# Attention and GEGLU block in one kernel: the last two groups in units of two head slots by 128 queries, and the first half of the last FFN beside the last exponentials

## The chip, the cores and the metric

The kernel runs on one core of a Trainium2 chip. The metric is the device time of one execution in microseconds (us). The engines are named as the profile names them: PE is TensorE (PEld its weight loads), DVE is VectorE, ACT is ScalarE, POOL is GpSimd, SP is the engine that issues DMAs.

## The reference

x has 2048 tokens of 512 bf16 values; 32 heads of 16; the FFN is 1792 wide.

```python
def _A_ref(x, wqkv, wo):                      # S = 2048, D = 512, H = 32, Dh = 16
    qkv = (x @ wqkv).reshape(B, S, 3, H, Dh).transpose(2, 0, 3, 1, 4)
    q, k, v = qkv[0], qkv[1], qkv[2]
    scores = jnp.einsum("bhqd,bhkd->bhqk", q, k) * (Dh ** -0.5)
    p = softmax(scores, axis=-1)
    o = jnp.einsum("bhqk,bhkd->bhqd", p, v)
    return o.transpose(0, 2, 1, 3).reshape(B, S, D) @ wo

def _B_ref(x, w_gate, w_up, w_down):
    return (gelu(x @ w_gate) * (x @ w_up)) @ w_down      # tanh form of Gelu

h  = x + _A_ref(layernorm(x), A_wqkv, A_wo)
h2 = h + _B_ref(layernorm(h), B_w_gate, B_w_up, B_w_down)
return h2
```

## The kernel before, in words

**A plan in Python.** Every instruction is recorded by `P.op` or `P.dma` (lines 96 and 112) with the buffers that it reads and writes; the plan works out the semaphore waits. So the order of the calls in Python is the order of each engine's queue, and what a queue holds is executed in that order.

**Groups, slots, units.** The 2048 queries are cut into eight groups of 256 tokens (`gi`), the 32 heads into eight slots of four heads (`slot`). A unit `ui` is one group and one slot, 64 in all (line 345). The four heads of a slot stand on four groups of 32 partitions, so that score matmuls use 32 rows of the PE array each, at tile positions 0, 32, 64 and 96.

**Two passes and the tick.** Softmax needs each row's maximum ahead of the exponential. In pass 1 (`p1_pair`, line 831, `p1_consume`, line 847) PE makes the scores with queries on partitions, two banks of 128x512 at a time, and DVE reduces them to maxima (L856); that pair is a *tick*, and a unit has 16 ticks. The negated maximum is written by `negm_pre` and `negm_post` (lines 878 and 894), through one DMA transpose per unit and one POOL addition (L905), into unused rows of the query operand. In pass 2 (`p2_tile`, line 914) PE makes the scores again, with keys on partitions: per unit eight key pairs `m` by four heads `g`, each a bank of two 256-wide matmuls (L921), from which ACT takes exp (L950, or in pairs of banks L938). Pass 2 is 24 ticks behind pass 1 (`P2_START`, line 982). After the last tick of pass 1 (1024) there are thus 24 ticks with pass 2 alone; here `dve_free` is set and DVE does the evacuations. `item_pv` (line 953) multiplies the exponentials by V, in four pieces from ticks 15 to 18 of a unit (`PV_T`): heads on four groups of 32 PSUM partitions, 17 columns each, the last one of which sums the row. The result goes through a DMA transpose (`o_turn`) and is divided on POOL (`o_norm`: L998, L1002).

**The dense stream.** All other matmuls are items in a queue (`Dense`, line 528): `prio` for what is due, `ready` for the rest, and `piece()` gives out one piece per tick, whose cost is counted in 512-wide matmuls. `startable` and `act_lag` hold an item back while ACT is thought to be late. If a tick's piece is under two such matmuls, `dummy` (L1410) fills the rest; in the last 24 ticks five in every two ticks are filled (`FILL_2`, line 1524). When all slots of a group are done, `post_onT` transposes the group's output, `item_oproj` does the out-projection and the residual, POOL the LayerNorm (`ln2_from_sums`), `post_hnT` transposes, and `add_ffn` queues seven `item_gate` and seven `item_up` (two chunks of 128 FFN columns by 256 tokens, L1198) and two `item_down` (L1250 and L1255). ACT evacuates gate and up; Gelu is a polynomial on POOL and a tanh on ACT (`gelu_chain`, L1178 and L1186 to L1190, the product L1242). A group's FFN runs while the next group's scores are worked on.

**The end.** The last group has no next one. `tail_a` (line 1275) transposes the first six slots of its output, `item_ofin` (line 1009) treats slot 6, and `tail_b` (line 1350) does the rest behind the last exponential: `tail_norm` and `tail_onT` for slot 7, the out-projection of both token tiles (L1361), statistics (L1364, L1365, L1369), reciprocal root on POOL (L1373), normalisation (L1375), transposes (`tail_hnT`), with up to 13 matmuls put in by `fill(FILL_LN)`, which are those of a queued `item_down` of group 6; then all seven gate and up tiles for 256 tokens with a real Gelu on ACT (L1211) and the product on DVE (L1227), the downs two steps behind, and the two stores (L1406).

## Time and profile before

| | |
|---|---|
| median of 3 runs | 1231.28 us (1231.07 to 1231.67) |
| the profiled execution's own time | 1231.23 us |
| its span, first to last instruction | 1229.3 us |
| last row maximum of pass 1 ends | 1176.8 us |
| last exponential ends | 1200.1 us |
| first gate matmul of the last FFN | 1207.85 us |
| busy share of the span | PE 90%, DVE 96%, ACT 97%, POOL 68% |

The times in the profile count from the span's start. A line number such as L856 is that of the kernel before. Matmul records hold the whole way through the array, so what a matmul costs in a row of many is read from the distance of their starts. "x8" in a row is eight instructions merged; the first number is the first one's start and the second the time up to the last one's end.

### The profile page before, as it was taken

What the parts mean: (1) busy time and instruction counts of PE and PEld (TensorE: products, weight loads), DVE (VectorE), ACT (ScalarE), POOL (GpSimd) and SP (SyncE); (2) the same over time, 40 slices, a digit from 0 to 9 for tenths busy, and PEclk for the clock granted to TensorE, in tenths of its full rate; (3) what the DMA queues carried; (4) which work ended last, traced back from release to release, by engine and by line L of the source; (5) the groups of instructions that cost most, each with busy time, mean ns of one, the idle gap of its engine ahead of it and who ended that gap; (6) DMA issues with size and microseconds to landing.
All of it is one profiled execution on the core that took longest, in us unless ns stands there. A gap on an engine that the chain in (4) does not pass through costs nothing.

```text
span 1229.3 us, 31435 instructions
## 1 busy us (share of the span) xinstructions
PE 1104.8 (90%) x12462; PEld 429.5 (35%) x12598; DVE 1175.8 (96%) x1111; ACT 1189.5 (97%) x2417; POOL 834.6 (68%) x1760
## 2 busy tenths in 40 slices
PE   7899988889998989898989989999888988889898
PEld 3233232233333333333332333333333333333335
DVE  8999999999999999999999999999999999999933
ACT  7899999999999999999999999999999999999993
POOL 7567684766776586757768477775867777548850
PEclk9999999999999999999999999999999999999999
DMA  4111114200010000100011000100001100010000
GB/s 153 27 34 27 29 26 136 87 10 9 8 27 21 14 9 8 31 21 7 11 25 18 17 11 7 28 21 13 10 8 26 27 8 11 18 32 10 8 19 14
DMA packets 68658, 31.54 MB, mean 26 GB/s; under 512 B 53920, under 2 KB 67488, under 8 KB 68512
## 3 DMA queue, kind: packets, MB, share of 16 engines
q1 hardware_dynamic: 68512, 29.52, 9.5%
q8 instruction: 101, 1.65, 0.5%
q14 instruction: 45, 0.37, 0.1%
HBM read 11.80 MB, written 2.10 MB: 11 GB/s over the span
## 4 chain that ended last, share of the span: by engine, by line
ACT 57%; DVE 29%; PE 8%; issue 3%; POOL 2%; DMA 0%; POOLq 0%; DVEq 0%
ACT PTM L950 32%; DVE PM L856 29%; ACT PTG L950 10%; ACT PTE L950 6%; PE pbank L1250 2%; ACT g_sb L685 2%; ACT u_sb L685 2%; ACT th_sb L1178 2%; PE pbank L841 1%; PE pbank L921 1%; PE pbank L1198 1%; ACT OB L685 1%; PE pbank L443 1%; DVE OA L853 1%; PE pbank L1410 1%
## 5 line engine op out<-in xcount | busy, mean ns | idle before, releaser
L856 DVE TENSOR_REDUCE PM<-pbank 128x2 f32<-128x1024 f32 x998 | 1135.9, 1212 | 8.3 <-PE pbank L921 3.8
L950 ACT ACTIVATE PTM<-pbank 128x512 bf16<-128x512 f32 x1357 | 731.9, 719 | 3.9 <-PE pbank L921 0.4
L921 PE MATMUL pbank<-QT,KT 32*128 32x256 bf16 x4096 | 503.0, 273 | 14.8 <-ACT PTM L950 7.6
L841 PE MATMUL pbank<-KT,QT 32*128 32x512 bf16 x2022 | 388.6, 384 | 31.5 <-DVE PM L856 11.8
L1410 PE MATMUL pbank<-ones_bf,ident 128*128 128x512 bf16 x708 | 221.4, 384 | 52.2 <-ACT PTM L950 22.5
L950 ACT ACTIVATE PTG<-pbank 128x512 bf16<-128x512 f32 x407 | 224.8, 704 | 1.7 <-PE pbank L921 1.3
L841 PEld LDWEIGHTS pbank<-KT,QT 32*128 32x128 bf16 x2022 | 97.9, 90 | 363.4 <-DVE PM L856 139.0
L921 PEld LDWEIGHTS pbank<-QT,KT 32*128 32x128 bf16 x4096 | 170.3, 92 | 75.9 <-ACT PTM L950 40.4
L950 ACT ACTIVATE PTE<-pbank 128x512 bf16<-128x512 f32 x236 | 139.3, 717 | 1.3 <-PE pbank L921 0.9
L964 PE MATMUL pbank<-PTM,VA 128*17 128x256 bf16 x2776 | 125.4, 274 | 1.5
L998 POOL TENSOR_TENSOR LINV<-OBT,negone 128x8 f32<-128x8 bf16 x62 | 103.5, 1670 | 2.7 <-DMA OBT<-OB 2.7
L1188 POOL TENSOR_TENSOR th_sb<-g_sb 128x512 f32<-128x512 f32 x49 | 51.0, 1041 | 76.5 <-ACT g_sb L685 76.5
L1410 PEld LDWEIGHTS pbank<-ones_bf,ident 128*128 128x128 bf16 x810 | 47.8, 97 | 149.1 <-ACT PTM L950 94.9
L964 PEld LDWEIGHTS pbank<-PTM,VA 128*17 128x17 bf16 x2776 | 60.0, 89 | 45.5 <-issue 29.8
L1198 PE MATMUL pbank<-hnT_l,wg_sb 128*128 128x256 bf16 x448 | 67.0, 275 | 4.1 <-ACT PTM L950 0.9
L1198 PE MATMUL pbank<-hnT_l,wu_sb 128*128 128x256 bf16 x448 | 67.1, 275 | 2.1
L1187 POOL TENSOR_TENSOR th_sb<-th_sb,g_sb 128x512 f32<-128x512 f32 x49 | 62.3, 1270 | 4.1
L1190 POOL TENSOR_TENSOR th_sb<-th_sb,g_sb 128x512 f32<-128x512 f32 x49 | 62.1, 1268 | 1.7
L1242 POOL TENSOR_TENSOR GUT<-th_sb,u_sb 128x512 bf16<-128x512 f32 x49 | 62.1, 1268 | 1.2
L1250 PE MATMUL pbank<-wd_sb,GUT 128*128 128x512 bf16 x209 | 57.7, 382 | 2.8 <-ACT PTM L950 1.3
L905 POOL TENSOR_TENSOR QT<-QT,STG 128x256 bf16<-128x256 bf16 x64 | 42.8, 669 | 23.0 <-DMA STG<-ST 22.3
L1186 POOL TENSOR_SCALAR th_sb<-th_sb 128x512 f32<-128x512 f32 x49 | 30.4, 620 | 39.7 <-ACT th_sb L1178 39.7
(168 smaller groups left out, 1130.2 us busy)
## 6 DMA issues: line engine op xcount, KB each, us to landing
QKS<-QKS SPq DMA_DIRECT2D x27, 112.0 KB, 2.1
x_sb<-in_A_x_dram SPq DMA_DIRECT2D x4, 512.0 KB, 5.7
xres<-in_A_x_dram SPq DMA_DIRECT2D x16, 128.0 KB, 2.3
out_dram<-out_sb SPq DMA_DIRECT2D x16, 128.0 KB, 1.7
wg_sb<-in_B_w_gate_dram SPq DMA_DIRECT2D x4, 448.0 KB, 4.3
wu_sb<-in_B_w_up_dram SPq DMA_DIRECT2D x4, 448.0 KB, 3.9
wd_sb<-in_B_w_down_dram SPq DMA_DIRECT2D x3, 512.0 KB, 4.3
STG<-ST SPq DMA_TRANSPOSE x64, 2.3
```

What stands on the lines that cost most here:

```text
L841: P.op("pe", lambda e, g=g, b=b: e.matmul(pbank[:, b, :], QT[32 * g:32 * g + 32, c, slot, 128 * qt:128 * qt + 128], KT[32 * g:32 * g + 32, ...
L856: P.op("dve", lambda e: e.tensor_reduce(out=PM[:, par, qt, kc, g:g + 2], in_=pbank[:, b:b + 2, :], axis=AX.X, op=ALU.max), reads=[("pb", b ...
L921: P.op("pe", lambda e, kt=kt, i=i: e.matmul(pbank[:, b, 256 * i:256 * i + 256], KT[32 * g:32 * g + 32, slot, 128 * kt:128 * kt + 128], QT[ ...
L950: P.op("act", lambda e, b=b, pi=pi: e.activation(out=PTt(pi), in_=pbank[:, b, :], func=ACT.Exp), reads=[("pb", b)], writes=[("PT", pi)], e ...
L964: P.op("pe", lambda e, g=g, kt=kt, pi=pi, i=i: e.matmul(pbank[32 * g:32 * g + 17, b, 0:256], VA[:, kt, 4 * slot + g, :], PTt(pi)[:, 256 * ...
L998: P.op("pool", lambda e: e.tensor_tensor(out=li, in0=o4[:, :, :, 16], in1=negone[:, 0:8].rearrange("p (q h) -> p q h", q=2), op=ALU.pow), ...
L1187: o(1.27, lambda e: e.tensor_tensor(out=ts_, in0=ts_, in1=gs, op=ALU.mult), [("th", par), ("g", par)])], then=done)
L1190: o(1.27, lambda e: e.tensor_tensor(out=ts_, in0=ts_, in1=gs, op=ALU.mult), [("th", par), ("g", par)])], then=poly_done)
L1198: P.op("pe", lambda e, dc=dc, fc=fc, i=i: e.matmul(pbank[:, b, 256 * i:256 * i + 256], w[:, dc, 128 * fc:128 * fc + 128], hT[:, dc, :], st ...
L1242: P.op("pool", lambda e: e.tensor_tensor(out=o_ap, in0=shp(ts_), in1=shp(us), op=ALU.mult), reads=[("th", par), ("u", par)], writes=o_keys ...
L1250: P.op("pe", lambda e: e.matmul(pbank[:, b, :], GUT[:, fc, 128 * k:128 * k + 128], wd_sb[:, fc, :], start=first, stop=last), reads=[("GUT" ...
L1410: P.op("pe", lambda e: e.matmul(pbank[:, b, :], ident[:], ones_bf[:, 0:512], start=True, stop=True), reads=["ident", "ones_bf"], writes=[( ...
```

## The change

It has three parts. **Units**: for groups 6 and 7 a unit is two neighbouring slots by 128 queries: first four units with the group's first 128 tokens (half 0), then four with the others. Pass 1 takes the second slot where it took the second 128 queries. In pass 2 a bank holds four 128-wide matmuls instead of two 256-wide ones, and `item_pv` has twice as many matmuls at half the width. The first 128 tokens of a group are so done four units ahead of the others. **Group 6**: out-projection, LayerNorm and FFN run for each half by itself, with gate and up tiles of four chunks by 128 tokens (four tiles per half, the last one with two chunks). **Group 7**: half 0's out-projection (`item_oprojA`) starts at tick 1024 with its LayerNorm on DVE; then its gate and up tiles (`item_raw`) run beside the last exponentials, and DVE copies them as they are, in fp32, over the query operand's memory that is no longer used (GA, UA). Behind the last exponential ACT takes Gelu of GA in place, POOL and DVE multiply by UA, and only the other 128 tokens go through the small steps, gate, up and down; the last down is split in two halves of 256 columns. The last unit's output is done in two parts: slot 6 (`PV_TL` 9 and 10) while slot 7's exponentials go on.

The diff, cut to what the text speaks of:

```diff
+PV_TL = (9, 10, 17, 18)
+DOWN_AT = 2
+A_LATE = True
+GH = 6
-FILL_LN = 13
+FILL_A = 2
...
+        GA = at("GA", [128, NFC, 128], FP32, 0)
+        UA = at("UA", [128, NFC, 128], FP32, NSLOT * 512 * 2)
...
-        units = [(gi, slot) for gi in range(NG) for slot in range(NSLOT)]
+        UB = GH * NSLOT
+        units = [(gi, slot) for gi in range(GH) for slot in range(NSLOT)] + [(gi, 2 * sp) for gi in range(GH, NG) for _ in range(2) for sp in range(NSLOT // 2)]
+        half = lambda ui: (ui - UB) // (NSLOT // 2) % 2
+        def part(ui, qh):
+            gi, slot = units[ui]
+            hf = gi % 2
+            return (slot, 2 * hf + qh) if ui < UB else (slot + qh, 2 * hf + half(ui))
...
         def p2_tile(ui, j, gp, jj, bank=None):
-            for i in range(2):
-                kt = 2 * m + i
-                P.op("pe", lambda e, kt=kt, i=i: e.matmul(pbank[:, b, 256 * i:256 * i + 256], ...
+            n, q0, kt0 = 2, 256 * hf, 2 * m
+            if ui >= UB:
+                slot, qt = part(ui, m // 4)
+                n, q0, kt0 = 4, 128 * qt, 4 * (m % 4)
+            qn = 512 // n
+            for i in range(n):
+                kt = kt0 + i
+                P.op("pe", lambda e, kt=kt, i=i: e.matmul(pbank[:, b, qn * i:qn * i + qn], KT[32 * g:32 * g + 32, slot, 128 * kt:128 * kt + 128],
+                                                          QT[32 * g:32 * g + 32, c, slot, q0:q0 + qn], start=True, stop=True, tile_position=(32 * g, 0)),
...
         def item_pv(...):
+                    n, c0, s_ = (2, 0, slot) if ui < UB else (4, 128 * (m // 4), slot + m // 4)
+                    qn = 512 // n
+                    for i in range(n):
+                        kt = 2 * m + i if ui < UB else 4 * (m % 4) + i
...
         def o_norm(gi, slots, ks, par, o4, key, busy):
+            if gi >= GH and not free:
+                defer(1, lambda: o_norm(gi, slots, ks, par, o4, key, busy))
+                return
...
-            pool.add([(1.45, inv), (0.31, mul)], then=over)
+            pool.add([(1.45, inv), (0.31, mul)], then=over, front=gi >= GH)
...
+            if gi == GL and A_LATE:
+                dense.add(item_oprojA, front=True, est=3, not_before=max(dense.now + 5, 16 * NU))
...
+        def item_oprojA(b):
+            for hc in range(4):
+                P.op("pe", ... e.matmul(pbank[:, b, :], OnT[:, 0, hc, :], wo_sb[:, hc, :], ...
+                if hc == 1:
+                    yield 2
+            P.op("pe", ... e.matmul(pbank[:, b, :], ident[:], hh, start=False, stop=True) ...
+            P.op("dve", ... e.bn_stats(out=stats2[:, t, :], in_=pbank[:, b, :]) ...
+            P.op("dve", ... e.tensor_copy(out=hh, in_=pbank[:, b, :]) ...
+            P.op("dve", ... e.bn_aggr ...
+            P.op("dve", ... e.tensor_scalar(out=rstd2[:, tt], in0=mv2[:, tt, 1], scalar1=EPS, ...
+            def rest():
+                P.op("dve", ... e.tensor_scalar(out=hn_sb[:, 0, :], in0=hh, ...
+                dense.add(item_hnA, front=True, est=1, not_before=dense.now + 1)
+            pool.add([(0.6, ... op=ALU.pow ...)], then=lambda: defer(1, rest), front=True)
...
+        def item_hnA(b):
+            (four transposes of hn_sb[:, 0], one DVE copy to hnT_l)
+            add_raw()
...
+        def half_mms(b, gi, k, t, w, nm, hr):
+            fcs = chunks(t)
+            for i, fc in enumerate(fcs):
+                for dc in range(4):
+                    P.op("pe", ... e.matmul(pbank[:, b, 128 * i:128 * i + 128], w[:, dc, 128 * fc:128 * fc + 128], hnT_l[gi % 2][:, dc, 128 * k:128 * k + 128], ...
+                if i == 1 and len(fcs) > 2:
+                    yield 2
...
+        def item_raw(b, t, w, nm, dst, key):
+            yield from half_mms(b, GL, 0, t, w, nm, [("hnT", GL % 2, 0)])
+            evac_act(dst[:, 4 * t:4 * t + n, :]..., pbank[:, b, 0:128 * n], ...)
+            raw_left[0] -= 1
+            return 2
...
         def tail_b():
+            while raw_left[0]:
+                dense.pause = 0
+                dense.piece()
+                run_deferred(tick, flush=True)
             P.op("act", ... func=ACT.Gelu_apprx_tanh ...)
+            for t in range(NTL):
+                raw_gelu(t)
+            raw_mult(0)
             while not a_done[0]:
                 fill(1)
             in_bank(tail_norm)
+            tail_a2()
             in_bank(tail_onT)
             fill(2)
             (out-projection, statistics and power for the second token tile alone)
+            raw_mult(1, "dve")
+            raw_mult(2)
+            raw_mult(3)
             (normalisation of the second token tile)
+            down_h(0, GL, 0)
+            for fc in chunks(0):
+                down_mm(0, GL, 0, fc)
+            fill(FILL_A)
+            tail_hnT(2, (0, 1), "act")
+            tail_hnT(3, (2, 3), "dve")
+            for fc in chunks(1):
+                down_mm(0, GL, 0, fc)
             while dense.busy():
                 ...
+            end_h()
+            for t in range(NTL):
+                tail_gate(gb[2 * t % 5], t)
+                tail_up(gb[(2 * t + 1) % 5], t)
+                if t == 0:
+                    for fc in range(8, NFC):
+                        down_mm(0, GL, 0, fc)
+                    (copy and store of the first 128 tokens)
+                if t >= 2:
+                    for q in range(2):
+                        end_mm(q, chunks(t - 2))
+            for q in range(2):
+                end_mm(q, range(4 * (NTL - 2), NFC))
+            (copies of 256 columns on DVE and ACT, one store each)
...
+            while not p1_ok and (cost or 0) < want:
+                c_ = dense.piece()
+                if not c_:
+                    break
+                cost = (cost or 0) + c_
```

In the last 24 ticks the queue may so give out several pieces per tick up to the five slots, queued items of group 6's down are put behind the gate and up tiles (`dense.ready.sort`), and `startable` lets an `item_down` start there. `JOINT`, the list of units in which one tick of pass 1 is saved, is as before.

447 lines of the change are left out of this document (269 added, 178 removed).

## Prediction

> **What bounds the kernel now.** I read the page first, then the chain of waits, the windows, the timeline of the last 50 us, and the list of waits.
>
> ```profile
> span 1229.3 us, 31435 instructions
> PE 1104.8 (90%) x12462; PEld 429.5 (35%) x12598; DVE 1175.8 (96%) x1111; ACT 1189.5 (97%) x2417; POOL 834.6 (68%) x1760
> ACT 57%; DVE 29%; PE 8%; issue 3%; POOL 2%; DMA 0%; POOLq 0%; DVEq 0%
> L856 DVE TENSOR_REDUCE PM<-pbank 128x2 f32<-128x1024 f32 x998 | 1135.9, 1212 | 8.3 <-PE pbank L921 3.8
> ```
>
> The row maxima (L856) keep VectorE busy from the start to 1176.8 us: 998 reductions and only 8.3 us of idle time before them. Up to there a tick of the schedule costs one reduction, about 1.14 us, and whatever else is done in it is free as long as it fits. What follows is the end, in four stages:
>
> ```profile
> core 0: us, PE busy (x) PEld busy (x) DVE busy (x) ACT busy (x) POOL busy (x), PEclk, DMA share, GB/s
> 886.00:1176.90 290.90, 259.01 (x3057) 102.15 (x3086) 288.71 (x257) 288.64 (x596) 208.68 (x428) 1.00 0.07 16
> 1176.90:1200.10 23.20, 21.99 (x268) 9.38 (x272) 1.97 (x4) 22.93 (x28) 10.55 (x16) 1.00 0.07 21
> 1200.10:1207.80 7.70, 7.46 (x55) 3.47 (x48) 4.25 (x13) 3.66 (x6) 0.70 (x1) 1.00 0.00 0
> 1207.80:1226.30 18.50, 18.35 (x139) 13.63 (x140) 5.26 (x8) 4.18 (x7) 0.00 (x0) 1.00 0.03 9
> ```
>
> Row one is the last two groups up to the last reduction. In row two only the exponentials are left (ACT 22.93 of 23.20 us, VectorE 1.97). In row three a chain of small steps passes from engine to engine, and row four is the FFN of the last 256 tokens with TensorE full (18.35 of 18.50 us). The time after the last exponential, some 29 us, is what the change works on.
>
> ```profile
> 1196.11 3.99 ACT L938 ACTIVATE PTM<-pbank 128x1024 bf16<-128x1024 f32 x4
> 1200.60 0.42 DVE L674 COPY OA<-pbank 128x256 f32<-128x256 f32 x1 [4.35 <-PE pbank L964]
> 1203.61 0.70 DVE L1364 BATCH_NORM_STATS2 stats<-pbank 128x6 f32<-128x512 f32 x1 [0.57 <-PE pbank L1361]
> 1204.22 0.68 DVE L1365 BATCH_NORM_STATS2 stats<-pbank 128x6 f32<-128x512 f32 x1
> 1204.82 0.30 DVE L1369 BATCH_NORM_AGGREGATE mv<-stats 128x2 f32<-128x6 f32 x2
> 1206.21 0.73 DVE L1375 TENSOR_SCALAR OnT<-xres,mv,rstd 128x512 bf16<-128x512 bf16 x2 [0.88 <-POOL rstd L1373]
> 1207.85 1.03 PE L1198 MATMUL pbank<-hnT_l,wg_sb 128*128 128x256 bf16 x8
> 1208.72 1.04 PE L1198 MATMUL pbank<-hnT_l,wu_sb 128*128 128x256 bf16 x8
> 1223.53 2.75 PE L1250 MATMUL pbank<-wd_sb,GUT 128*128 128x512 bf16 x12
> 1226.32 0.60 ACT L1403 ACTIVATE out_sb<-pbank 128x512 bf16<-128x512 f32 x1 [2.87 <-PE pbank L1250]
> ```
>
> Eight 256-wide matmuls start 0.87 us after the eight before them (1207.85 to 1208.72): 0.109 each. Twelve 512-wide ones span 2.75 with a last one of 0.38, so (2.75 - 0.38)/11 = 0.216 each. Stage four is 112 x 0.109 + 28 x 0.216 = 18.3 us, which is what it takes.
>
> **The change, part by part.** The sums are made against the profiled execution: 1231.23 us, of which the span is 1229.3; the runs' median is 1231.28, so I count the two as one.
>
> *FFN at the end (a).* Of the 256 tokens only 128 are left behind the last exponential. A 128-wide matmul with a weight load of its own has a row at the kernel's start, the transposes:
>
> ```profile
> 10.15 1.06 PE L421 MATMUL pbank<-ident,xn_sb 128*128 128x128 bf16 x16
> L421 PE MATMUL pbank<-ident,xn_sb x16: 219/219/219, 10.2 to 11.0; 128*128 128x128 bf16 x16
> ```
>
> (1.06 - 0.22)/15 = 0.056 us each. So gate and up are 112 x 0.056 = 6.2 us, down for these tokens is two halves of 256 columns, 28 x 0.109 = 3.0, and six of the fourteen 512-wide downs of the other 128 tokens come behind the first gate and up, 6 x 0.216 = 1.3. That makes 10.5 in place of 18.3: **-7.8**. The Gelu of each tile and its product (0.60 and 0.69 us in the trace) stay beside the next tile's 1.8 us of matmuls. The Trainium skill ("TensorE: Matmul & The Clock Gate", section "Back-to-back issue gap") gives about 81 ns per matmul for a sustained stream of load and matmul pairs at 128 columns; the row says 56, and by 81 the term would be an estimated 2.9 us smaller.
>
> *The chain of small steps (b).* From the copy at 1200.60 to the first gate matmul at 1207.85 it takes 7.25. One token tile instead of two takes out the second statistics (0.61, from 1203.61 to 1204.22), one aggregate (0.15), one output matmul (0.22), and about half of two small copies (0.2): -1.2. The chain gains, on TensorE between the transposes of hn and the first gate, four downs and two 256-wide residual matmuls, 1.1 us, where 1.0 us of transposes and copies lay partly beside two 512-wide ones: +0.4. The four Gelu calls on stored values (about 0.6 each) start behind the table load that the kernel has there already, and run beside the statistics. The product that VectorE now does (about 0.69) stands ahead of the normalisation in its queue; it fits the 0.88 us in which VectorE waits for GpSimd's power, and costs up to 0.7 if its Gelu is late. **-0.8**.
>
> *The end (c).* The last copies are 256 wide instead of 512 (0.60 for 512): **-0.2**; the first 128 tokens' store leaves earlier.
>
> *Beside the last exponentials (d).* TensorE takes on the out-projection and 112 gate and up matmuls; VectorE copies eight tiles (six of 512 columns at about 0.69, two of 256 at 0.42) and does a LayerNorm: some 8 us in 23 of which it uses 2. What does TensorE do there now?
>
> ```profile
> 1176.89 0.41 PE L921 MATMUL pbank<-QT,KT 32*128 32x256 bf16 x8 [0.78 <-DVE PM L856]
> 1177.23 1.25 PE L1410 MATMUL pbank<-ones_bf,ident 128*128 128x512 bf16 x5
> 1178.42 0.41 PE L921 MATMUL pbank<-QT,KT 32*128 32x256 bf16 x8
> 1182.43 0.61 PE L964 MATMUL pbank<-PTM,VA 128*17 128x256 bf16 x16
> 1176.90:1200.10 23.20, 8.00 (x30) 2.61 (x33) 1.00 0.07 21
> 1182.80 0.67 ACT L1178 ACTIVATE th_sb<-th_sb 128x512 f32<-128x512 f32 x1
> ```
>
> The fifth row is line 1410 alone: 30 recorded dummies, put in to fill five 512-wide slots in every two ticks. Two ticks are 1.89 us for ScalarE (24 pair exponentials in 22.7 us). A round of TensorE is 0.34 for the scores and 1.18 for five dummies, 1.52, so 0.37 is free. With real pieces of two slots the loop overshoots to six: 24 matmuls of 128, 1.33 + 0.1, and the round is 1.77. The scores come as sixteen 128-wide matmuls instead of eight 256-wide. Their eight now span 0.41 with one of 0.27, so two rounds of four at once; I take four rounds of 0.056, the same 0.22 us, as the lower end, and 13 starts one behind the other, 0.72, as the upper. The upper gives a round of 2.27, 0.38 too long, in six to seven rounds of raw pieces: 2.5 us. The wait for the LayerNorm ahead of item_hnA stands in TensorE's queue with the next scores behind it, up to 1 us, against exponentials' input that is made one or two pairs ahead. Between 0 and +3.5, nearer the concurrent row: **+0.8**. The late tanh at 1182.80, about 0.5 in the row of exponentials, may go, because half of group 6's FFN starts four units sooner: **-0.3**, between 0 and -0.5.
>
> *Do the pieces fit (e)?* 24 ticks hold 60 to 70 slots. Output of units 62 and 63 needs 12, the out-projection 5, the gate and up tiles 28, three transposing items 3: 48. They cannot start before the LayerNorm, near tick 1029, and the four ticks of unit 62's output stand in between; from my count the last tile falls three or four ticks before the end. A down of group 6 (15 x 0.216 = 3.2 us) that is still queued is what would tip it over. Part of it would find room in the small steps. **+0.4**, between 0 and +3.2.
>
> *The last two groups up to 1176.9 (f).* The reductions, the exponentials and the stats per unit keep number and size; a unit takes two head slots of 128 queries where it took one of 256. SP issues the same DMA transposes, one pair per unit; the first tokens' OnT transpose and residual load leave four units sooner, past nothing that waits. GpSimd's two steps of the output norm now go ahead of queued Gelu steps, at most 2 us of delay for these, with 208.68 of 290.90 us busy there. Scores and output matmuls become twice as many at half the width. Output matmuls run four at once (16 in 0.61, one of 0.27: four rounds of 0.11), so 32 in eight rounds of 0.056 cost the same. For the scores the addition lies between 0 and 0.2 us a tick. The slack:
>
> ```profile
> PEld pbank L841 <- DVE PM L856: 32.3, 74, 0.6
> PEld pbank L1410 <- ACT PTM L950: 27.2, 68, 0.9
> PEld pbank L841 <- issue: 25.3, 100, 0.4
> PEld pbank L841 <- ACT PTM L950: 17.9, 48, 1.1
> PEld pbank L841 <- ACT PTG L950: 6.4, 20, 0.5
> PEld pbank L1410 <- ACT PTG L950: 5.9, 16, 0.4
> PEld pbank L841 <- ACT PTE L950: 4.3, 10, 1.3
> PEld pbank L1410 <- ACT PTE L950: 3.2, 8, 0.8
> ```
>
> In 256 ticks the loader waits 97.2 us for VectorE or ScalarE, 244 times. A wait that ends by "issue", so for no one, has a mean of 0.25, which I take as the unavoidable part: 97.2 - 61 = 36 us, or **0.14 us a tick**, is slack. A cost below that is hidden, except in the four ticks of each unit that carry output matmuls. ScalarE has none to spare (288.64 of 290.90 busy); FFN of group 6 in halves gives it one more small evacuation and tanh per kind, and one or two output copies move ahead of 1176.9: about 1 us. **+0.8**, between 0 and +8.
>
> Sum: -7.8 - 0.8 - 0.2 + 0.8 - 0.3 + 0.4 + 0.8 = -7.1, so **1224.1 us**.
>
> **The rivals.**
>
> *A, the score matmuls lose their concurrency (slower).* Four 128-wide matmuls in a row stand on one row group. If the next group's can't start past them, a tick's eight take 8 x 0.056 = 0.45 for 0.22: +0.22 against 0.14 slack. The 0.08 left over, times 256, is +20; in the last stretch sixteen take 0.9 for 0.22, and rounds of 2.4 instead of 1.89 add some 6. With the -8 of the end: 1231 - 8 + 20 + 6 = 1249. It decides from 0.04 us a tick, 10 us in all. Against it: eight matmuls in two rounds show that TensorE looks at least two deep, and half the additions in a tick lie beside the 512-wide L841. 0.08.
>
> *B, 128-wide matmuls cost 81 instead of 56 ns, the page's rule.* Here: +2.9 at the end, up to 2.9 beside the exponentials, and 4 x 0.025 = 0.1 a tick, inside the slack: 1224.1 + 5 = 1229. The transposes speak against it, but run at full height, not on 32 rows. 0.07.
>
> *C, TensorE becomes the bound beside the exponentials.* Terms d and e at their upper ends: +2.7 + 2.8 = 1229.6 at most, half of it 1227. What is left over of the tiles is then done ahead of the last small steps. It is likely in part, since TensorE's fill goes from five slots to six. 0.20.
>
> *D, the change doesn't do what it says:* the LayerNorm of the first tokens comes too late, and most gate and up tiles run after the last exponential anyway, 6.2 us on the path: 1230. The 20 ticks that are left speak against it. 0.05.
>
> **How the numbers follow.** Forecast 0.60, A 0.08, B 0.07, C 0.20, D 0.05. 0.2%, 2.5 us, is about what the measurement tells from no change: faster is below 1228.8. Forecast, nearly all of C and half of B give 0.80; the rest of B and C, D and the weak end of A give 0.11 for the same; slower 0.09. The range goes from 1220.5 (terms d to f at their lower ends, and the small steps half a microsecond better) to 1230 (C and B).
>
> **What would show it.** (a) From the first gate matmul at the end to the last down about 10.5 us, and 128-wide matmuls 0.056 apart. (b) About 6.5 from the last OA copy to that gate. (d) Pair exponentials without gaps over some 23 us; almost no L1410 there. (e) No gate or up tile of the first tokens behind the last exponential. (f) The last reduction within 1 us of 1176.8, and sixteen score matmuls in about 0.4. I am wrong if the last reduction comes over 5 us later (A), or if the end stays over 14 us.

## The result, and the profile after

The changed kernel takes 1225.08 us (median of 4 runs, 1224.82 to 1226.58) and the kernel before, on the same chip, 1231.43 us (4 runs, 1231.07 to 1231.67). The ratio is 0.9951, 95% interval 0.9934 to 0.9968: faster by 6.35 us, where 1224.1 us was forecast. The profiled execution is the slowest of the four, 1226.58 us with a span of 1224.5, so its span is 4.7 us shorter than before, and not 6.35. A second profile of the same kernel, on another chip, is used beside it ("after, again", below).

The page of the changed kernel: its head and the row maxima.

```profile
span 1224.5 us, 36091 instructions
PE 1131.4 (92%) x14847; PEld 477.4 (39%) x14847; DVE 1180.8 (96%) x1120; ACT 1189.8 (97%) x2421; POOL 840.3 (69%) x1772
L867 DVE TENSOR_REDUCE PM<-pbank 128x2 f32<-128x1024 f32 x998 | 1136.4, 1212 | 8.3 <-PE pbank L943 3.8
```

There are some 4700 instructions more, nearly all of them 128-wide matmuls and their weight loads. The row maxima (now L867) keep number, mean and idle time. What bounds the first 1177 us has not changed.

The windows of the changed kernel, cut at its own stages: span, then busy time of PE, PEld, DVE, ACT and POOL, then the granted clock. The last row is that of the dummies alone (L1587) beside the exponentials.

```profile
886.00:1177.30 291.30, 271.70 (x5026) 147.78 (x5025) 289.03 (x257) 289.98 (x600) 212.27 (x435) 1.00 0.09 18
1177.30:1201.00 23.70, 22.20 (x531) 15.25 (x532) 8.58 (x19) 22.57 (x28) 9.87 (x18) 1.00 0.06 15
1201.00:1211.00 10.00, 7.52 (x95) 3.66 (x93) 4.81 (x11) 4.32 (x8) 4.17 (x4) 0.88 0.04 13
1211.00:1222.10 11.10, 11.10 (x147) 9.86 (x145) 2.92 (x5) 2.78 (x5) 0.00 (x0) 0.96 0.04 13
1177.30:1201.00 23.70, 2.42 (x8) 0.69 (x8) 1.00 0.06 15
```

Row four is what the change is for: 11.1 us of full TensorE where there were 18.5. Row two shows where the rest went: VectorE is busy 8.58 us beside the exponentials instead of 1.97, and of 30 recorded dummies 8 are left. Row three is the surprise: the stage of small steps, forecast shorter, went from 7.7 to 10 us.

The timeline of the changed kernel, from the first scores of the last stretch to the end. In these rows OA is the copy of the last unit's output, GUT holds the products of Gelu and up, and OnT, in the normalisation and the transposes behind it, is the normalised h.

```profile
1177.37 0.44 PE L943 MATMUL pbank<-QT,KT 32*128 32x128 bf16 x16 [1.01 <-DVE PM L867]
1182.66 1.07 PE L1292 MATMUL pbank<-hnT_l,wg_sb 128*128 128x128 bf16 x16 [0.52 <-DVE hnT_l L1215]
1184.15 7.52 ACT L960 ACTIVATE PTM<-pbank 128x1024 bf16<-128x1024 f32 x8 [0.70 <-PE pbank L943]
1196.21 0.42 DVE L685 COPY UA<-pbank 128x256 f32<-128x256 f32 x1 [0.24 <-PE pbank L1292]
1197.04 3.93 ACT L960 ACTIVATE PTM<-pbank 128x1024 bf16<-128x1024 f32 x4
1198.69 2.55 PE L1391 MATMUL pbank<-wd_sb,GUT 128*128 128x512 bf16 x11
1201.08 0.38 PE L1396 MATMUL pbank<-xres,ident 128*128 128x512 bf16 x1
1201.84 0.62 PE L989 MATMUL pbank<-PTM,VA 128*17 128x128 bf16 x32
1202.51 0.29 DVE L685 COPY OA<-pbank 128x128 f32<-128x128 f32 x1 [0.33 <-PE pbank L989]
1206.03 0.93 POOL L1543 TENSOR_TENSOR rstd<-rstd,nhalf 128x1 f32<-128x1 f32 x1 [1.68 <-DVE rstd L1542]
1206.94 1.99 POOL L1490 TENSOR_TENSOR GUT<-GA,UA 128x512 bf16<-128x512 f32 x2
1207.07 1.27 DVE L1547 TENSOR_SCALAR OnT<-xres,mv,rstd 128x512 bf16<-128x512 bf16 x1 [0.52 <-POOL rstd L1543]
1208.40 0.54 PE L1469 MATMUL pbank<-ident,OnT 128*128 128x128 bf16 x4 [2.08 <-DVE OnT L1547]
1208.74 1.91 PE L1391 MATMUL pbank<-wd_sb,GUT 128*128 128x512 bf16 x4
1210.87 1.56 PE L1292 MATMUL pbank<-hnT_l,wg_sb 128*128 128x128 bf16 x16
1215.36 1.06 PE L1292 MATMUL pbank<-hnT_l,wu_sb 128*128 128x128 bf16 x16
1216.25 1.06 PE L1292 MATMUL pbank<-hnT_l,wg_sb 128*128 128x128 bf16 x16
1222.18 0.38 ACT L1580 ACTIVATE out_sb<-pbank 128x256 bf16<-128x256 f32 x1 [2.25 <-PE pbank L1515]
```

Three places are to be seen. The last exponential ends at 1200.97 (1197.04 + 3.93), and the matmuls that need it are behind eleven downs and a residual matmul of group 6 (1198.69 to 1201.46): the last OA copy comes 1.54 us behind the exponential, where it was 0.50. The normalisation of 512 columns takes 1.27 us; before, two of them took 0.73. And from 1208.4 on matmuls take longer than elsewhere: four downs 1.91 us instead of 1.03, sixteen gates 1.56 instead of 1.06. The granted clock there, in the third row of the windows, is 0.88.

The last exponential's time, the last OA copy, the first gate matmul behind it and the end of the last matmul cut each kernel's end into the same stages. In microseconds, from the timelines; "main" is the 256 row maxima of the last 16 units:

| | main | last maximum to last exp | to last OA copy | to first gate | to last matmul | to the end |
|---|---|---|---|---|---|---|
| before | 294.23 | 23.26 | 0.50 | 7.25 | 18.43 | 3.00 |
| after | 294.92 | 23.66 | 1.54 | 8.36 | 11.27 | 2.39 |
| after, again | 294.95 | 23.74 | 1.61 | 7.21 | 10.77 | 2.38 |

The second profile has the same 2.08 us wait on TensorE, and its clock stays up there:

```profile
1208.04 1.27 DVE L1547 TENSOR_SCALAR OnT<-xres,mv,rstd 128x512 bf16<-128x512 bf16 x1 [0.52 <-POOL rstd L1543]
1209.37 0.40 PE L1469 MATMUL pbank<-ident,OnT 128*128 128x128 bf16 x4 [2.08 <-DVE OnT L1547]
1210.69 1.06 PE L1292 MATMUL pbank<-hnT_l,wg_sb 128*128 128x128 bf16 x16
1210.70:1221.50 10.80, 10.70 (x147) 9.48 (x145) 2.92 (x5) 2.78 (x6) 0.00 (x0) 1.00 0.04 14
```

So 1.65 us of the first profile (8.36 - 7.21 and 11.27 - 10.77) belong to the lower clock of that execution; the other three executions of the changed kernel took 1.4 to 1.8 us less. The second profile is the one to set against the forecast. It has a fall of the clock of its own, at the kernel's start, which the term-by-term account below comes to.

### The profile page after: what moved, and what is told of

It reads as the page before. It is cut to its first block, busy times and chain, and to the rows that moved or that the text cites. A ratio compares the mean times of both kernels' runs of the same rounds, so it can differ in the third digit from the quotient of the medians.

```text
span 1224.5 us, 36091 instructions
## 1 busy us (share of the span) xinstructions
PE 1131.4 (92%) x14847; PEld 477.4 (39%) x14847; DVE 1180.8 (96%) x1120; ACT 1189.8 (97%) x2421; POOL 840.3 (69%) x1772
## 4 chain that ended last, share of the span: by engine, by line
ACT 54%; DVE 35%; PE 8%; issue 2%; POOL 1%; POOLq 0%; DVEq 0%
DVE PM L867 34%; ACT PTM L972 30%; ACT PTG L972 9%; ACT PTE L972 5%; PE pbank L1391 2%; ACT g_sb L696 2%; ACT th_sb L1262 2%; ACT u_sb L696 2%; PE pbank L852 1%; PE pbank L943 1%; ACT PTM L960 1%; ACT OB L696 1%; PE pbank L455 1%; PE pbank L1587 1%; PE pbank L1292 1%
## 5 line engine op out<-in xcount | busy, mean ns | idle before, releaser
L867 DVE TENSOR_REDUCE PM<-pbank 128x2 f32<-128x1024 f32 x998 | 1136.4, 1212 | 8.3 <-PE pbank L943 3.8
L943 PE MATMUL pbank<-QT,KT 32*128 32x256 bf16 (+1 forms) x5120 | 505.4, 250 | 14.3 <-ACT PTM L972 6.9
L852 PE MATMUL pbank<-KT,QT 32*128 32x512 bf16 x2022 | 388.7, 384 | 26.0 <-DVE PM L867 10.5
L1587 PE MATMUL pbank<-ones_bf,ident 128*128 128x512 bf16 x778 | 237.7, 384 | 29.7 <-ACT PTM L972 5.3
L943 PEld LDWEIGHTS pbank<-QT,KT 32*128 32x128 bf16 x5120 | 205.1, 92 | 68.1 <-ACT PTM L972 38.7
L989 PE MATMUL pbank<-PTM,VA 128*17 128x256 bf16 (+1 forms) x3470 | 126.1, 252 | 1.6
L1030 POOL TENSOR_TENSOR LINV<-OBT,negone 128x8 f32<-128x8 bf16 x63 | 105.1, 1668 | 11.4 <-DMA OBT<-OB 11.1
L1587 PEld LDWEIGHTS pbank<-ones_bf,ident 128*128 128x128 bf16 x778 | 45.6, 97 | 132.5 <-ACT PTM L972 83.5
L1272 POOL TENSOR_TENSOR th_sb<-g_sb 128x512 f32<-128x512 f32 (+1 forms) x50 | 51.1, 1023 | 66.2 <-ACT g_sb L696 66.2
L1271 POOL TENSOR_TENSOR th_sb<-th_sb,g_sb 128x512 f32<-128x512 f32 (+1 forms) x50 | 62.4, 1249 | 3.9
L1274 POOL TENSOR_TENSOR th_sb<-th_sb,g_sb 128x512 f32<-128x512 f32 (+1 forms) x50 | 62.3, 1246 | 1.8
L1270 POOL TENSOR_SCALAR th_sb<-th_sb 128x512 f32<-128x512 f32 (+1 forms) x50 | 30.5, 611 | 37.3 <-ACT th_sb L1262 37.3
L767 POOL TENSOR_SCALAR QT<-QKS,qmask 128x512 bf16<-128x512 bf16 x30 | 46.9, 1567 | 13.1 <-ACT QKS L696 12.2
L1347 PE MATMUL pbank<-hnT_l,wg_sb 128*128 128x256 bf16 x336 | 51.2, 275 | 3.3 <-ACT PTM L972 0.7
L1383 POOL TENSOR_TENSOR GUT<-th_sb,u_sb 128x512 bf16<-128x512 f32 x42 | 53.3, 1268 | 1.3
```

The lines of the kernel that those rows point to most:

```text
L852: P.op("pe", lambda e, g=g, b=b: e.matmul(pbank[:, b, :], QT[32 * g:32 * g + 32, c, slot, 128 * qt:128 * qt + 128], KT[32 * g:32 * g + 32, ...
L867: P.op("dve", lambda e: e.tensor_reduce(out=PM[:, par, qt, kc, g:g + 2], in_=pbank[:, b:b + 2, :], axis=AX.X, op=ALU.max), reads=[("pb", b ...
L943: P.op("pe", lambda e, kt=kt, i=i: e.matmul(pbank[:, b, qn * i:qn * i + qn], KT[32 * g:32 * g + 32, slot, 128 * kt:128 * kt + 128], QT[32 ...
L989: P.op("pe", lambda e, g=g, kt=kt, pi=pi, i=i, s_=s_, c0=c0, qn=qn: e.matmul(pbank[32 * g:32 * g + 17, b, c0:c0 + qn], VA[:, kt, 4 * s_ + ...
L1030: P.op("pool", lambda e: e.tensor_tensor(out=li, in0=o4[:, :, :, 16], in1=negone[:, 0:4 * nq].rearrange("p (q h) -> p q h", q=nq), op=ALU. ...
L1271: o(1.27, lambda e: e.tensor_tensor(out=ts_, in0=ts_, in1=gs, op=ALU.mult), [("th", par), ("g", par)])], then=done)
```

## The experiments

**Theories.** T: the gain is one of place; 112 gate and up matmuls of the first tokens moved from behind the last exponential to beside it. Against the forecast two things were lost. T1: the down of group 6 is done at the wrong moment, ahead of the matmuls that the last exponential releases (1.0 us). T2: GpSimd's product (L1490) runs beside VectorE's normalisation and lengthens it (0.86 us, 1.27 less the 0.41 of one tile before). Rivals: the place does not matter and the smaller forms do it; for T1 and T2, that something else ends last as soon as the thing named is gone (TensorE, which has the same work to do in any order); for the slack in the tick, that TensorE has much more or much less of it than the 0.14 us of the forecast. All kernels below are the changed kernel with an edit more: an order, the number of dummies, or, in one, the number of groups with the new units.

| | median us | ratio to before | main | to last exp | to OA | to gate | to last matmul | to the end |
|---|---|---|---|---|---|---|---|---|
| e0_after | 1225.28 | 0.9942 [0.9930, 0.9955] | 294.95 | 23.74 | 1.61 | 7.21 | 10.77 | 2.38 |
| e1_late | 1230.29 | 0.9986 [0.9976, 0.9995] | 295.48 | 22.86 | 0.51 | 13.66 | 10.77 | 2.39 |
| e2_gh7 | 1230.13 | 0.9981 [0.9972, 0.9990] | 295.39 | 24.17 | 1.54 | 9.94 | 10.78 | 2.69 |
| e3_hold | 1225.12 | 0.9939 [0.9927, 0.9952] | 295.06 | 23.67 | 0.51 | 7.91 | 10.77 | 2.39 |
| e4_pool | 1223.88 | 0.9932 [0.9920, 0.9944] | 295.50 | 23.67 | 1.54 | 6.35 | 10.77 | 2.38 |
| e6_hna | 1225.85 | 0.9946 [0.9932, 0.9959] | 295.26 | 22.90 | 2.40 | 7.21 | 10.77 | 2.38 |
| e8_dummy | 1236.13 | 1.0031 [1.0020, 1.0043] | 305.70 | 23.82 | 1.54 | 7.21 | 10.77 | 2.39 |
| e10_pre | 1223.84 | 0.9930 [0.9916, 0.9943] | 295.04 | 23.73 | 0.51 | 6.96 | 10.77 | 2.38 |
| e12_all | 1222.83 | 0.9925 [0.9912, 0.9939] | 295.51 | 22.90 | 0.51 | 6.96 | 10.77 | 2.39 |
| e13_dve | 1222.31 | 0.9924 [0.9910, 0.9937] | 294.63 | 22.90 | 0.51 | 6.63 | 10.77 | 2.38 |

Differences under 1 us between these kernels are not told by the medians, whose intervals overlap. The stages tell them: the same code repeats within some 0.1 us in every column but "main", where the profiles with the same work lie between 294.63 and 295.51.

**The changed kernel again** (e0_after, no edit).

> The changed kernel itself once more, unchanged, beside the others on their chip, and for a second profile. In the first profile TensorE's granted clock is 0.88 in the 10 us behind the last exponential, and its span, 1224.5 us, is 1.5 us above the other executions' 1222.8 to 1223.1. If that clock dip belongs to the 2.1 us in which TensorE waits for the normalisation and comes only in some executions: a profile without it ends near 1223.0, with the normalisation still at 1.27 us and about 1.5 us between the last exponential and the copy of OA. Ratio to before 0.995.

Measured: 1225.28 us, 0.9942. This is the second profile above. The small steps stay at 7.21 us without the slower clock, so the forecast's "about 6.5" fails by itself. The span, 1223.8, is not down at the 1223.0 that was expected: in this execution the clock fell too, but at the kernel's start, and that cost 0.99 us (see the account below).

**The first tokens' gate and up behind the last exponential again** (e1_late; both places that sort the queue are changed alike).

```diff
-                raws += [(item_raw, (t, wg_sb, "wg", GA, "GA"), 1, 16 * NU), (item_raw, (t, wu_sb, "wu", UA, "UA"), 1, 16 * NU)]
+                raws += [(item_raw, (t, wg_sb, "wg", GA, "GA"), 1, 16 * NU + 24), (item_raw, (t, wu_sb, "wu", UA, "UA"), 1, 16 * NU + 24)]
-                dense.ready.sort(key=lambda it: it[0] is item_down)
+                dense.ready.sort(key=lambda it: it[0] is item_raw)
```

> The changed kernel, but the gate and up tiles of the last group's first 128 tokens (item_raw) may start only behind the last exponential; the queued down of group 6 no longer stands behind them. Theory T (the gain is 112 matmuls of 0.056 us that left the path): they are back on it, 6.2 us, less up to 1 us because group 6's down now runs earlier and the last output matmuls don't queue behind it: 1230 to 1231.5 us against 1225.1. Rival U (what is behind the last exponential is bound by the small steps, and TensorE has idle time there that would take most of the tiles): 1226 to 1228. Below 1226 neither holds.

Measured: 1230.29 us, 0.9986. The timeline has the first of the moved tiles behind the last exponential, which ends at 1200.54, and eight of them one after the other:

```profile
1200.93 1.07 PE L1292 MATMUL pbank<-hnT_l,wg_sb 128*128 128x128 bf16 x16
1207.38 0.62 PE L1292 MATMUL pbank<-hnT_l,wu_sb 128*128 128x128 bf16 x8 [0.27 <-DVE UA L685]
```

The small steps take 13.66 us instead of 7.21, 6.45 more, and that is about the 6.2 us of 112 x 0.056. The whole loses some 5, within what T had named, since two things come back: the exponentials end 0.9 us sooner after the last maximum, and the last OA copy stands 0.51 behind them again, the down having run earlier. T holds: most of the gain is the place of these 112 matmuls. What is left of the change in this kernel, the narrower forms among it, brings 1.7 us (1230.29 against 1231.96 on its chip).

**Group 6 with whole units and one FFN** (e2_gh7: `GH = 7` instead of 6).

> The changed kernel with only group 7 in units of two slots by 128 queries; group 6 has its units, its LayerNorm and its FFN in one piece as before the change. If group 6's halves matter because its FFN, 30 downs among it (6.5 us), is else still queued in a stretch whose TensorE is full: slower than the changed kernel by 3 to 6 us, ratio to before about 0.998 to 1.000. If group 6's halves only cost (half of the 0.7 us by which the last 256 ticks grew): 0.3 to 0.4 us faster than the changed kernel, ratio 0.9945.

Measured: 1230.13 us, 0.9981, as much as with the first tokens' tiles late. The timeline shows group 6 arriving late at the end: its last tanh is at 1188.68 still, and twelve downs stand between the transposes of hn and the first gate.

```profile
1188.68 0.63 ACT L1262 ACTIVATE th_sb<-th_sb 128x512 f32<-128x512 f32 x1
1210.09 2.75 PE L1391 MATMUL pbank<-wd_sb,GUT 128*128 128x512 bf16 x12
```

So the halves of group 6 are not a side matter. They are what lets its downs run ahead of or beside the last exponentials, and without them the 24 ticks hold the first tokens' tiles only at the price of group 6's downs behind (small steps 9.94 instead of 7.21, exponentials 0.4 longer). All the stages together account for 3.9 us of the 4.85 by which the median lies above e0_after's; the profiled execution, 1228.99 us, was itself 1.1 below the median.

**One more 512-wide slot in each tick of the last 16 units** (e8_dummy).

```diff
-                want = 2
+                want = 3 if tick >= 16 * UB else 2
```

> The changed kernel with one more 512-wide dummy slot per tick of pass 1 in the last two groups (three instead of two where the queue gives nothing). Up to 0.216 us more of TensorE per tick in 256 ticks, wherever the piece given out is under three. The prediction's slack of 0.14 us a tick, and what follows it, is tested: if a tick has just about that slack, 0.05 to 0.1 us a tick come out, 12 to 25 us: 1237 to 1250. If TensorE has more room (waits that end by nobody are slack too): under 3 us, below 1228. Above 1250 there is less slack than was worked out.

Measured: 1236.13 us, 1.0031. The dummies (L1587, with their weight loads counted in the second pair of brackets) over the last 256 ticks, in this kernel and in e0_after:

```profile
882.70:1188.40 305.70, 100.84 (x332) 31.93 (x404) 1.00 0.08 18
```

```profile
883.20:1178.10 294.90, 46.87 (x147) 10.19 (x178) 1.00 0.08 18
```

The loads went from 178 to 404: 226 x 0.216 = 48.8 us of TensorE were added, and the stage grew by 305.70 - 294.95 = 10.75. The other 38 us were hidden: 0.148 us per tick on the mean of all 256, or 0.168 for each added dummy. The time is just under the 1237 to 1250 that were expected, so there was a little more room than that. The forecast's 0.14 came from the loader's waits in the kernel before. Its way of reading them (waits for VectorE and ScalarE, less 0.25 for each) can be tried on the kernel that the dummies were added to: the same kinds of rows in e0_after, over the same 256 ticks, add up to 72.6 us in 204 waits, which leaves 21.6 us or 0.08 a tick, about half of what was hidden. So the slack is of the size that the forecast had, but the agreement of 0.148 with 0.14 is partly luck, and the reading by waits is not confirmed.

**The down waits for the last output matmuls** (e3_hold: a down may start only if all of it fits ahead of the next due item; `FILL_A` 2 to 13, so that it is done in the small steps).

```diff
-... self.now + (min(3, self.ready[0][2]) if dve_free[0] else ...) <= lim
+... self.now + ((self.ready[0][2] if self.ready[0][0] is item_down else min(3, self.ready[0][2])) if dve_free[0] else ...) <= lim
```

> The changed kernel, but group 6's last down may not start beside the exponentials unless it can end before the last output matmuls are due, and up to 13 slots (instead of 2) are filled while the normalisation is waited for. In the changed kernel's trace that down (11 matmuls and the residual, 1198.69 to 1201.3 us) holds the last output matmuls back: the copy of OA starts 1.54 us after the last exponential ends, 0.50 before the change. If that order is the cause, the distance goes back to about 0.6 and the time falls by 0.9 to 1.1 us, to about 1224.0; TensorE's idle 2.1 us ahead of the hn transposes takes the down. If the down only moves its 3.4 us to a place that ends last too: no change, 1225.1, or up to 1 us slower.

Measured: 1225.12 us, 0.9939.

```profile
1204.49 3.41 PE L1391 MATMUL pbank<-wd_sb,GUT 128*128 128x512 bf16 x15 [0.26 <-POOL GUT L1490]
1206.28 1.28 DVE L1547 TENSOR_SCALAR OnT<-xres,mv,rstd 128x512 bf16<-128x512 bf16 x1 [0.52 <-POOL rstd L1543]
1208.17 0.39 PE L1469 MATMUL pbank<-ident,OnT 128*128 128x128 bf16 x4
```

The cause was right, as the OA copy is 0.51 behind the last exponential again. The gain was not there: the small steps grew from 7.21 to 7.91. OnT is ready at 1207.56 (1206.28 + 1.28), but TensorE is on the fifteen downs and what belongs to them, and takes the transposes at 1208.17, without a wait. What was late in one place is late in the next: 1.1 us gained, 0.7 lost.

**GpSimd's second product before the power, not beside the normalisation** (e4_pool).

```diff
             raw_mult(0)
+            raw_mult(2)
...
             raw_mult(1, "dve")
-            raw_mult(2)
-            raw_mult(3)
...
             tail_hnT(3, (2, 3), "dve")
+            raw_mult(3, "dve")
```

> The changed kernel, but GpSimd's second product of stored Gelu and up (1.27 us) stands ahead of the reciprocal root in its queue instead of behind it, and the third, half-width one goes to VectorE behind the hn copies. In the changed kernel's trace the normalisation L1547 takes 1.27 us for one token tile, 0.37 before the change, and ends 0.1 us after GpSimd's product that runs beside it. If VectorE is held up by that GpSimd product: the normalisation takes about 0.4 us and the time falls by 0.8 to 0.9 us, to about 1224.2. If it is slow for another reason (its operands, or ScalarE's copy of the same tile): still 1.27, and no change.

Measured: 1223.88 us, 0.9932.

```profile
1203.71 2.49 POOL L1490 TENSOR_TENSOR GUT<-GA,UA 128x512 bf16<-128x512 f32 x2 [3.97 <-ACT GA L1486]
1207.71 0.41 DVE L1546 TENSOR_SCALAR OnT<-xres,mv,rstd 128x512 bf16<-128x512 bf16 x1 [0.52 <-POOL rstd L1544]
1208.18 0.40 PE L1469 MATMUL pbank<-ident,OnT 128*128 128x128 bf16 x4 [1.22 <-DVE OnT L1546]
```

The same instruction on the same data takes 0.41 instead of 1.27 us when GpSimd does nothing beside it, and TensorE's wait falls from 2.08 to 1.22: 0.86 both times. T2 holds, and the small steps are at 6.35. That is close to what the forecast had for them, but it is measured behind an OA copy that still comes 1.54 us late, which gives the Gelu calls and GpSimd's products 1.0 us more ahead of the small steps. In the three kernels below in which the copy comes at 0.51, these steps do not get under 6.63.

**The transposes of hn two ticks later** (e6_hna), against the 0.70 us that ScalarE waits ahead of 1184.15 in the changed kernel.

```diff
-                dense.add(item_hnA, front=True, est=1, not_before=dense.now + 1)
+                dense.add(item_hnA, front=True, est=1, not_before=dense.now + 3)
```

(the gate and up items are allowed from the next tick on, `max(16 * NU, dense.now + 1)`)

> The changed kernel, but the transposes of the first tokens' normalised h (item_hnA) are put two ticks later into TensorE's queue and the first gate tile one tick behind them, so that the next scores go ahead of them. In the changed kernel's trace ScalarE waits 0.70 us at 1184.15 for scores that stand behind these transposes. The gap should go, and the last exponential end 0.5 to 0.7 us sooner than in the changed kernel. Whether the time follows is open: the gate tiles end later, so all of group 6's last down (14 instead of 11 matmuls) stands ahead of the last output matmuls, 0.65 us. Theory T1 (the down ends last there): no change, within 0.3 us of the changed kernel. Theory T2 (the exponentials do): 0.6 us faster.

Measured: 1225.85 us, 0.9946.

```profile
1180.93 10.21 ACT L960 ACTIVATE PTM<-pbank 128x1024 bf16<-128x1024 f32 x11
1198.72 2.97 PE L1391 MATMUL pbank<-wd_sb,GUT 128*128 128x512 bf16 x13 [0.16 <-DVE UA L685]
```

The eleven exponentials run without a gap and the stretch is 22.90 instead of 23.74: the wait for the LayerNorm, with the next scores behind it in TensorE's queue, was the 0.7 us. But everything on TensorE is that much later, the down too, and the last OA copy is 2.40 behind the last exponential instead of 1.61. Again a gain of 0.8 in one stage is paid in the next: by the stages this is theory T1, no change. The median is 0.6 above e0_after's, which the times alone do not tell.

**Setting a down aside when output work is due** (e10_pre): the piece of the dense queue that is a down is put by while the due item runs, and taken up again behind it; `FILL_A` 7; and the order of products of e4_pool.

```diff
-                self.gen = None
+                self.gen, self.held = None, []
...
-                    if self.gen is None:
+                    if dve_free[0] and self.gen is not None and self.prio and self.cur is item_down and min(it[3] for it in self.prio) <= self.now and (self.held.append((self.gen, self.bank, self.cur)) or setattr(self, 'gen', None)) or self.gen is None:
...
-                        self.gen = None
...
+                        self.gen, self.bank, self.cur = self.held.pop() if self.held else (None, self.bank, self.cur)
```

> The changed kernel with two orders changed. An item_down beside the exponentials is set aside when output matmuls fall due, and goes on behind them, with 7 instead of 2 slots filled in the wait for the normalisation; and GpSimd's second product stands ahead of the reciprocal root, the third goes to VectorE. If both waits found in the trace add up (last output matmuls behind the down: 1.0 us; normalisation beside GpSimd's product: 0.9 us), and the rest of the down fits TensorE's idle time: 1.7 to 1.9 us below the changed kernel on the same chip, ratio to before about 0.9937 for 0.9951. If the small steps are then bound by TensorE's sum of work (as holding the whole down back showed no gain): 0.9 us, as for the second order alone.

Measured: 1223.84 us, 0.9930: 1.4 us below e0_after on the same chip, short of the 1.7 to 1.9 that were expected if both waits added up. The OA copy is at 0.51, the normalisation at 0.41, but the small steps are 6.96 and not 6.35:

```profile
1202.92 2.50 POOL L1490 TENSOR_TENSOR GUT<-GA,UA 128x512 bf16<-128x512 f32 x2 [3.90 <-ACT GA L1486]
1204.83 1.14 DVE L1490 TENSOR_TENSOR GUT<-GA,UA 128x512 bf16<-128x512 f32 x1
1205.37 1.01 POOL L1544 TENSOR_TENSOR rstd<-rstd,nhalf 128x1 f32<-128x1 f32 x1
```

The statistics are ready 1.0 us sooner after the last exponential, while the Gelu calls are tied to that exponential and the table load. So GpSimd's two products end at 1205.42, and the power, behind them in its queue, starts only then; VectorE's own product takes 1.14 beside them, and it was 0.68.

**All three orders at once** (e12_all: e10_pre and e6_hna).

> The kernel after with three orders of its own work changed: a down in progress is set aside for due output work (as in e10_pre), the product on VectorE no longer shares its normalisation with GpSimd's (as in e4_pool), and item_hnA asks for its LayerNorm two ticks later (as in e6_hna). If the 0.70 us gap at item_hnA and the down ahead of the last output matmuls are the two costs that the change left at the end, both go together: the exponentials after the last reduction take about 22.9 us instead of 23.7, the last OA copy stays 0.51 behind the last exponential instead of 2.40 as in e6_hna, and the time is 0.6 to 0.8 below e10_pre, ratio to the kernel before about 0.992 to 0.9925. Rival: what starts two ticks later on TensorE moves raw tiles or downs behind the last exponential, so the gain is paid back between the last OA copy and the first gate matmul (over 7.5 us there instead of 6.96), and the ratio stays at 0.993.

Measured: 1222.83 us, 0.9925 (0.9912 to 0.9939). Exponentials 22.90, OA copy 0.51, small steps 6.96. The 0.83 us of the exponentials, which e6_hna paid back, is kept whole on top of e10_pre.

**The second product on VectorE** (e13_dve: e12_all, with `raw_mult(2, "dve")` behind the copies of hn and not on GpSimd).

> e12_all with GpSimd's second product given to VectorE, behind the copies of hn: GpSimd does only the first product and then the power. If it is that second product (2.50 us for two in a row, 1202.77 to 1205.27 in e12_all) that keeps the power waiting from 1204.76 to 1205.24 and lengthens VectorE's product to 1.14 us, the power starts right behind the addition of eps, the product returns to 0.68, and the way from the last OA copy to the first gate matmul falls from 6.96 to 6.3 to 6.5 us: about 0.5 us, ratio to the kernel before about 0.992. Rival: TensorE is full there with the down that was set aside (its last residual matmul ends at 1206.43 in e12_all), or the third product on VectorE comes too late for its downs: the way stays at 6.8 to 7.0 and the time does not move. 0.5 us is under what the times alone tell; the stages of the profile decide.

Measured: 1222.31 us, 0.9924 (0.9910 to 0.9937).

```profile
1204.27 0.68 DVE L1490 TENSOR_TENSOR GUT<-GA,UA 128x512 bf16<-128x512 f32 x1
1204.44 0.93 POOL L1543 TENSOR_TENSOR rstd<-rstd,nhalf 128x1 f32<-128x1 f32 x1 [0.80 <-DVE rstd L1542]
1205.48 0.41 DVE L1545 TENSOR_SCALAR OnT<-xres,mv,rstd 128x512 bf16<-128x512 bf16 x1 [0.52 <-POOL rstd L1543]
1205.65 0.38 PE L1396 MATMUL pbank<-xres,ident 128*128 128x512 bf16 x1
1206.08 0.39 PE L1469 MATMUL pbank<-ident,OnT 128*128 128x128 bf16 x4
```

The power starts at once, the product is back at 0.68, and the normalisation starts 4.73 us behind the OA copy instead of 5.18. Of that 0.45 the gate keeps 0.33: 6.63, short of the 6.3 to 6.5 expected. The rest is the rival's: OnT is ready at 1205.89, but a residual matmul and a dummy are still on TensorE, and the transposes start at 1206.08. This is the lowest median of the kernels; its ratio is not told apart from that of e12_all, only its stages are. With 1222.31 against 1231.78 us on its chip it gains 9.5 us where the change as made gains 6.4 to 6.9.

## Why the prediction was right, point by point

The forecast was 7.1 us less than the profiled 1231.23. Set against the second profile (1223.8 of span, 5.4 less than before), term by term, with the forecast first and the measured after it:

- **(a) the FFN at the end, -7.8:** 10.77 us from the first gate to the last down, 10.5 expected (its parts, added again, make 10.6); -7.66. Sixteen 128-wide matmuls start 0.89 us after the sixteen before them (1215.36 and 1216.25 in the first profile), 0.056 each, the price taken from the transposes at the kernel's start. The rival with 81 ns from the Trainium skill ("TensorE: Matmul & The Clock Gate", section "Back-to-back issue gap") is out: this stream of load and matmul pairs at 128 columns takes 56.
- **(b) the small steps, 7.25 to 6.5, -0.8:** this step failed. They stayed at 7.21. The forecast put the right product in VectorE's wait for the power, where it fits (0.68 us, L1490), and looked only at VectorE's queue. It did not price GpSimd's own next product running beside the normalisation. That cost 0.86 us, and with it taken away the steps take 6.35 (e4_pool). With the OA copy as early as the forecast had it, they take 6.96 with the same order (e10_pre) and 6.63 at best (e13_dve): there GpSimd's products come too late and then TensorE is still busy with the down.
- **(c) the end, -0.2:** -0.62. The last copy is 0.38 instead of 0.60, as expected; the other 0.4 us lie behind it, at the store, whose size the term had left out; 0.3 of them show in the rows. The DMA views of the last 15 us, before and after, end with the time from issue to landing:

```profile
out_dram<-out_sb SPq DMA_DIRECT2D x2, 128.0 KB, 1.8
```

```profile
out_dram<-out_sb SPq DMA_DIRECT2D x2, 64.0 KB, 1.5
```

- **(d) beside the last exponentials, +0.8 - 0.3:** +0.48. The late tanh is gone, as said, and the wait ahead of item_hnA with scores behind it cost 0.7, within the "up to 1 us"; e6_hna shows it. TensorE had the room: 8 dummies are left of 30.
- **(e) do the pieces fit, +0.4:** +1.11, by the mechanism named and at another price. The gate and up tiles did fit, the last one's copy at 1196.21 being 4.8 us ahead of the last exponential's end. The down of group 6 was still queued, and it stood ahead of the last output matmuls. The forecast saw its cost as work left over (3.2 us at most, most of which finds room); what it cost was its place in the queue.
- **(f) the last two groups, +0.8:** +0.72, with a caution. The profiles of kernels with this same work spread over 0.9 us in this stage (294.63 to 295.51), so the term is told only to that. That a cost of some 0.1 us a tick is hidden is confirmed (e8_dummy); the 0.14 itself, read from waits, is not.

The rest of the difference, +0.56, lies ahead of the last 16 units, where the two kernels do the same. It belongs to that execution and not to the change: its granted clock fell to 0.50 between 23 and 26 us, so that the row for 20 to 60 us has a mean of 0.96,

```profile
20.00:60.00 40.00, 34.33 (x220) 12.23 (x224) 37.52 (x35) 32.73 (x65) 24.58 (x55) 0.96 0.09 26
```

and from its fourth to its ninth row maximum it takes 6.87 us, where the kernel before and the first profile take 5.88. That is 0.99 lost, of which 0.47 had been gained by an earlier start. Without the fall the spans differ by 6.4, as the medians do (6.35 and, on the second chip, 6.85).

So the sum stood, with b and e together 1.5 us too good and c 0.4 too bad: the stages that the change touches give -6.0 where -7.1 was forecast. That the miss is no larger is in part luck, as c was wrong the other way. The lower end of the range is off by its own terms, which add up to 1221.4 and not 1220.5; the measured time is well inside either.

**Rivals.** A is out: sixteen score matmuls of 128 columns in the last stretch take 0.44 us, where eight of 256 took 0.41; one behind the other they would have taken 0.9. No stage grew by the 20 us. C is out as a bound on the exponentials, whose stretch grew by 0.4 to 0.5. But a part of it is what term e cost: work left over on TensorE stood ahead of the last output matmuls, 1.1 us. B's 1229 would be up to 1229.9 by its own parts. D is out by the windows and by e1_late, which is what D would have looked like: 1230.29, where D had 1230.

## What to carry to other kernels

At the end of a kernel each stage has another bound, and the engines' queues are in order. So a gain in one stage is kept only if what it moves does not stand ahead of the next stage's first instruction: e3_hold and e6_hna each gained about 1 us and lost 0.7 to 0.8 of it again. With the down set aside and the order of the products changed as well (e12_all), 2.2 of the 2.8 us that the three are worth one by one were kept. When work is put into an engine's wait, look at what the other engines do in the same microsecond too, and not only at that engine's own queue.

## What the runs showed of the hardware that was not expected

- VectorE and GpSimd wait for each other in some pairs of instructions. A bf16 normalisation of 128x512 in SBUF took 0.41 us with GpSimd idle, and 1.27 to 1.28 behind a GpSimd fp32 product of 1.26 that had started 0.13 us earlier (1206.94 and 1207.07 in the first profile), in each of the seven profiles with that order. It is nearly all waiting: the product itself kept its 1.26. The other way round, the power on GpSimd took 0.93 in e13_dve when VectorE's product had started 0.17 us ahead of it, and 0.58 with VectorE idle (the power of the first tokens in e12_all):

```profile
1181.12 0.58 POOL L1207 TENSOR_TENSOR rstd<-rstd,nhalf 128x1 f32<-128x1 f32 x1 [1.30 <-DVE rstd L1202]
```

  The Trainium skill ("SBUF — State Buffer", section "SBUF: two separate sides") describes a port pair that the two engines share, as an exclusive lock held for a whole instruction by whichever starts first, with the other blocked and not slowed in proportion; of VectorE's instructions it names those in a two-port mode or with two inputs in SBUF. The rows with the products agree with it; the prediction had not weighed it. One pair does not agree. The normalisation of the first tokens is the same instruction, and a power on GpSimd starts 0.07 us ahead of it and lasts 1.64, and still it takes 0.41, in all eleven profiles of the changed kernel and its variants:

```profile
1181.21 1.64 POOL L1030 TENSOR_TENSOR LINV<-OBT,negone 128x8 f32<-128x8 bf16 x1
1181.28 0.41 DVE L1204 TENSOR_SCALAR OnT<-xres,mv,rstd 128x512 bf16<-128x512 bf16 x1 [0.69 <-POOL rstd L1207]
```

  So not every GpSimd instruction holds VectorE up, and the runs do not show what sets the two cases apart.
- The granted clock fell in one execution of the changed kernel, behind a TensorE wait of 2.08 us that the change brought: 0.54 from 1208.3 to 1211.0, and 0.77 in the two microseconds after it.

```profile
1208.30:1211.00 2.70, 2.60 (x12) 1.37 (x13) 0.34 (x2) 0.38 (x1) 0.63 (x1) 0.54 0.00 0
1211.00:1213.00 2.00, 2.00 (x31) 2.00 (x29) 0.00 (x0) 0.53 (x1) 0.00 (x0) 0.77 0.00 0
```

  The same wait of 2.08 us stands in e0_after, e1_late, e6_hna and e8_dummy, and there the clock stayed at 1.00. In e0_after it fell instead at 23 us, at a wait of 1.03. Why it fell in the one place and not in the others is open; it cost 1.65 and 0.99 us.
- 128-wide score matmuls on four groups of 32 rows keep their concurrency though four in a row stand on the same rows: sixteen take the 0.44 us above. The forecast had taken this as its lower end, with rival A against it.
